# A list scheduler in the source that orders all engines between token tiles 2 and 95 of an attention and feed-forward kernel

## The chip, the cores and the metric

The kernel runs on one core of a Trainium2 chip. A core has a matrix engine (PE, with PEld for its weight loads), a vector engine (DVE), a scalar engine (ACT), GpSimd (POOL) and SyncE (SP), which issues nearly all DMA transfers here. Each engine works through its own list of instructions in the order of the program; an instruction whose inputs or buffers are not ready holds up everything behind it on its engine. The metric is the device time of one execution in microseconds (us). Before the change it is 1622.03 us, the median of three runs (1621.46 to 1624.27).

## What is computed

```python
# x: 4 x 12480 x 128, inducing: 32 x 128, w_in: 128 x 2048, w_out: 2048 x 128
def mab(q, kv):
    s = scale * (q @ kv.transpose(0, 2, 1))
    a = np.exp(s - s.max(-1, keepdims=True))
    a /= a.sum(-1, keepdims=True) + 1e-09
    return a @ kv
h = mab(I, x)          # 32 rows attend to all tokens of a batch
y = mab(x, h)          # each token attends to those 32 rows
z = y @ w_in
out = np.maximum(0.01 * z, z) @ w_out
```

## The kernel before, in words

**Tiles.** The 49920 tokens are cut into 98 tiles (`tiles`): 96 of 512 tokens and two of 384, which hold the ends of two batches each. A batch has six groups of 2048 tokens (four tiles each) and a rest of 192 (`GROUPS`).

**The main work.** A token's row of `y` is its 32 attention weights A times `h`, so z = A (h w_in), and the first product of the feed-forward part has a depth of 32 only. PE is therefore used as four independent row groups of 32 rows. One *slot* is one tile with one of the 16 column blocks f of z. It has three first products (`ffn_first`, weights `hwhi`, `hwlo`, data `A4`; high and low halves of fp32 numbers) on row group f % 4, into a PSUM bank `ph`; then ACT writes `ghi` = relu (L853) and DVE `glo`, the low half (L856), and after that the bank is free. For every fourth f (`FAR`) ACT writes `g` (L846), which frees the bank, and POOL makes `ghi` and `glo` from it (L848, L849). Then come twelve second products, three on each row group, each with its own accumulator bank. All of these go through `quarter` (L878). A tile is 16 slots and three linear products (the 0.01 z part): 243 products. At its end `gather` adds the four banks (ACT copy L1160, DVE sum L1163, POOL sum L1167) and `store` transposes (L924) and writes out.

**The side work** prepares the next batch and the next A: loads of x (`xc` L321, `xr` L311), DVE transposes into `xT` (L440), scores for `h` (L335, L347, L366), values (L486, L459), the weights' product (L655), and for each group `second` (L335, then DVE, POOL and ACT on `y`) and `stack`: ACT casts A to `both` (L736), POOL makes its low half (L741), and SP copies it to the four row groups of `A4` (L755). `both` has one buffer, so the next cast needs all four tiles' copies out of it done. The side products use all 128 rows of PE; such a stretch between two L878 products is called a *cluster* here.

**What sets the order.** Tiles 0, 1 and 97 run on the whole array (L904). For tiles 2 to 96 four generators (`row_group`) take turns, one product each. `row_group` sets a place for each slot's first products, `AHEAD` = 4 slots ahead of its second products (8 for `FAR`), row group r lags by r slots, and `glo` is issued `LATER` = 4 turns after `ghi`. Once per slot `next_slot` steps each lane of the side work by one piece (`others`), and `cluster` issues waiting side products when one has waited 10 slots. PSUM banks come from one list of eight, freed after a fixed number of turns. No durations are known to it.

## Time and profile before

| | |
|---|---|
| median of three runs | 1622.03 us |
| the profiled execution's own time | 1625.5 us |
| its span, first to last instruction | 1623.7 us |
| mean granted TensorE clock | 0.984 |
| DVE busy | 1157.0 us (71%) |
| ACT busy | 1068.4 us (66%) |
| POOL busy | 943.3 us (58%) |
| the chain that ended last | PE 82%, DVE 6%, POOL 4%, issue 3%, ACT 2% |

A row of a timeline has the start in us from the span's start, the duration in us, engine, line, operation, output<-inputs and shapes; in brackets stands how long the engine sat idle before it, and what ended that. A row of the waits names the waiting instruction, the one that released it, the sum in us, how often, and the longest. PE's matmuls are pipelined: one row group starts a product about every 0.23 us, while each row shows about 0.39 us. A few matmul records are missing from the trace.

### The profile page before, as it was taken

The page shows a single profiled execution, that of the slowest core. Times are in us where ns is not written, and L with a number is a line of the kernel's source. Part 1 is how long each engine was busy: PE and PEld are TensorE (multiplying, and loading weights), DVE is VectorE, ACT ScalarE, POOL GpSimd, SP SyncE. Part 2 cuts the span into 40 slices and gives each one's busy share as a digit, 9 for nine tenths or more (in the row PEclk, how much of TensorE's full clock was granted, in tenths as well). Part 3 has the DMA queues.
Part 4 walks back from the last instruction along what each step waited for, and adds up shares of the span by engine and source line. Part 5 has one row for each costly group of instructions (what it writes and reads, how often), then busy time and mean ns, then how long its engine had stood idle before and what let it go on. Part 6 is the DMA issues. An engine that isn't in the chain of part 4 may idle for free.

```text
span 1623.7 us, 59550 instructions
## 1 busy us (share of the span) xinstructions
PE 1571.7 (97%) x25047; PEld 1339.5 (82%) x25047; DVE 1157.0 (71%) x2046; ACT 1068.4 (66%) x1957; POOL 943.3 (58%) x963
## 2 busy tenths in 40 slices
PE   7999999999989999999998999999999999999997
PEld 5678777787877888888887878887888899999996
DVE  6677778767767777867675778776767676776764
ACT  6456656666756667766675567666666667777773
POOL 2046555556656655556665565655666666666663
PEclk9899999999999999999999999999999999999998
DMA  7154545522354446423225346542222232333321
GB/s 263 16 112 84 109 94 94 117 56 46 59 107 75 86 90 141 113 48 58 48 57 109 72 97 124 107 111 48 53 58 44 49 63 52 57 58 61 61 48 21
DMA packets 400700, 128.46 MB, mean 79 GB/s; under 512 B 373136, under 2 KB 375600, under 8 KB 400432
## 3 DMA queue, kind: packets, MB, share of 16 engines
q1 hardware_dynamic: 399328, 124.50, 38.0%
q8 instruction: 197, 3.23, 0.8%
q14 instruction: 71, 0.58, 0.1%
q10 hardware_dynamic: 1104, 0.15, 0.1%
HBM read 48.94 MB, written 25.56 MB: 46 GB/s over the span
## 4 chain that ended last, share of the span: by engine, by line
PE 82%; DVE 6%; POOL 4%; issue 3%; ACT 2%; SPq 1%; DMA 1%; ACTq 0%; DVEq 0%; POOLq 0%
PE bank L878 75%; PE bank L335 3%; DVE glo L856 2%; POOL glo L849 2%; PE bank L904 2%; PE bank L459 1%; POOL ghi L848 1%; DVE part L1163 1%; SPq L755 1%; ACT ghi L853 1%; DMA A<-both 1%; POOL y L710 1%; PE bank L366 0%; POOL y L696 0%; DVE e L347 0%
## 5 line engine op out<-in xcount | busy, mean ns | idle before, releaser
L878 PE MATMUL bank<-ghi,w_hi 32*128 32x512 f32 (+1 forms) x6080 | 1294.8, 393 | 2.2 <-DVE glo L856 1.7
L878 PE MATMUL bank<-glo,w_hi 32*128 32x512 f32 x6080 | 1293.9, 393 | 0.2 <-DVE glo L856 0.2
L878 PE MATMUL bank<-ghi,w_lo 32*128 32x512 f32 (+1 forms) x6080 | 1292.0, 393 | 0.0
L878 PE MATMUL bank<-A,hwhi 32*128 32x512 f32 (+1 forms) x3394 | 1140.0, 394 | 28.8 <-DVE glo L856 15.4
L856 DVE SCALAR_TENSOR_TENSOR glo<-bank,ghi 128x512 fp32r<-128x512 f32 x1184 | 792.4, 680 | 306.4 <-ACT ghi L853 301.0
L853 ACT ACTIVATE ghi<-bank 128x512 fp32r<-128x512 f32 x1184 | 703.1, 598 | 325.2 <-PE bank L878 306.6
L878 PEld LDWEIGHTS bank<-ghi,w_hi 32*128 32x128 f32 x6080 | 842.1, 184 | 51.1 <-issue 14.3
L878 PEld LDWEIGHTS bank<-ghi,w_lo 32*128 32x128 f32 x6080 | 847.4, 184 | 27.8
L878 PEld LDWEIGHTS bank<-glo,w_hi 32*128 32x128 f32 x6080 | 843.6, 184 | 28.6 <-DVE glo L856 0.6
L878 PEld LDWEIGHTS bank<-A,hwhi 32*128 32x128 f32 x3394 | 581.0, 185 | 90.1 <-DVE glo L856 42.4
L878 PE MATMUL bank<-A,hwlo 32*128 32x512 f32 (+1 forms) x1697 | 640.2, 390 | 0.0
L849 POOL TENSOR_TENSOR glo<-g,ghi 128x512 fp32r<-128x512 f32 (+1 forms) x384 | 495.9, 1291 | 30.7
L848 POOL CAST ghi<-g 128x512 fp32r<-128x512 f32 (+1 forms) x384 | 234.6, 611 | 417.2 <-ACT g L846 356.8
L878 PEld LDWEIGHTS bank<-A,hwlo 32*128 32x128 f32 x1697 | 305.8, 185 | 8.3
L846 ACT ACTIVATE g<-bank 128x512 f32<-128x512 f32 (+1 forms) x384 | 229.4, 597 | 124.8 <-PE bank L878 120.6
L1167 POOL TENSOR_TENSOR part<-part 128x512 f32<-128x512 f32 (+1 forms) x95 | 122.6, 1291 | 103.9 <-DVE part L1163 103.9
L1163 DVE TENSOR_TENSOR part<-bank,part 128x512 f32<-128x512 f32 (+1 forms) x190 | 129.2, 680 | 33.5 <-PE bank L878 21.0
L1160 ACT COPY part<-bank 128x512 f32<-128x512 f32 (+1 forms) x190 | 110.5, 581 | 26.1 <-PE bank L878 24.8
L924 DVE STREAM_TRANSPOSE osb<-part 128x512 f32<-128x512 f32 (+1 forms) x95 | 65.9, 694 | 0.0
L440 DVE STREAM_TRANSPOSE xT<-xc 128x512 f32<-128x512 f32 x72 | 50.2, 697 | 0.0
L741 POOL TENSOR_TENSOR both<-aT,both 128x512 fp32r<-128x512 f32 x24 | 31.1, 1295 | 29.2 <-ACT both L736 25.1
L690 DVE STREAM_TRANSPOSE y<-bank 128x512 f32<-128x512 f32 (+1 forms) x28 | 18.1, 647 | 21.3 <-PE bank L335 21.3
(120 smaller groups left out, 643.6 us busy)
## 6 DMA issues: line engine op xcount, KB each, us to landing
A<-both SPq DMA_DIRECT2D x376, 128.0 KB, 2.4
xr<-in_x_dram SPq DMA_DIRECT2D x96, 256.0 KB, 4.7
out_dram<-osb SPq DMA_DIRECT2D x382, 64.0 KB, 2.3
xc<-in_x_dram SPq DMA_DIRECT2D x288, 64.0 KB, 2.7
raw<-in_moe_w_in_dram SPq DMA_DIRECT2D x4, 512.0 KB, 6.6
raw<-in_moe_w_out_dram SPq DMA_DIRECT2D x4, 512.0 KB, 7.5
A<-both SPq DMA_DIRECT2D x48, 16.0 KB, 1.8
out_dram<-osb SPq DMA_DIRECT2D x48, 8.0 KB, 1.8
```

Source lines behind the costliest of these rows:

```text
L335: nc.tensor.matmul(dst, lhsT, rhs, start=True, stop=True)
L440: nc.vector.transpose(t[:, j, :], blk.rearrange("p n c -> p (n c)"))
L846: nc.scalar.activation(g[:, :n], ph[:, :n], AF.Relu)
L848: nc.gpsimd.tensor_copy(ghi[:, :n], g[:, :n])
L849: nc.gpsimd.tensor_tensor(out=glo[:, :n], in0=g[:, :n], in1=ghi[:, :n].bitcast(F32), op=ALU.subtract)
L853: nc.scalar.activation(ghi[:, :n], ph[:, :n], AF.Relu)
L856: nc.vector.scalar_tensor_tensor(out=glo[:, :n], in0=ph[:, :n], scalar=0.0, in1=ghi[:, :n].bitcast(F32), op0=ALU.max, op1=ALU.subtract,)
L878: nc.tensor.matmul(dst, w[32 * r : 32 * r + 32], x[32 * r : 32 * r + 32], start=start, stop=stop, tile_position=(32 * r, 0),)
L924: nc.vector.transpose(osb[:, :n], total[:, :n])
L1160: nc.scalar.copy(part[:, :n], po[:, :n])
L1163: nc.vector.tensor_tensor(out=part[:, :n], in0=po[:, :n], in1=part[:, :n], op=ALU.add)
L1167: nc.gpsimd.tensor_tensor(out=total[:, :n], in0=total[:, :n], in1=part[:, :n], op=ALU.add)
```

## The change

The kernel's arithmetic and its instructions' shapes stay. Between tiles 2 and 96 the fixed slots go, and a list scheduler that runs while the program is written takes their place. It keeps a clock for ACT, DVE, POOL and SP, the time at which each row group is free, the time at which each bank comes free, and the estimated end of each DMA, all in ns from constants in the source. At each step it takes what can start first: a product (`option`), a queued job of an engine (`best`), or a piece of a side lane, which gives way to queued jobs by `YIELDING`. First products may run up to ten slots ahead (`GB` = 10 buffers of `ghi` and of `glo`; before 7 and, for `FAR`, 3). Which slots go to POOL is no longer every fourth: `relu` sends a slot there when POOL would be done 1200 ns ahead of need. Side products are put in by `clustered`, by age or when PE would idle. `quarter` is L988 now, relu L975, `glo` on DVE L978 and on POOL L1216 and L1218, the cast to `both` L856.

```diff
-    FAR = 3
-    XB = 3
-    LATER = 4
-    FURTHER = 4
-    GB = 7
-    AHEAD = 4
-    LAG = 1
+    GB = 10
+    SLOT = 868.0
+    QUARTER = 231.6
+    SIGNAL = 35.0
+    DRAINED = 200.0
+    TURNED = 200.0
+    LANDED = 2300.0
+    RELU, LOW, COPIED, ADDED, BLOCKS = 599.0, 690.0, 585.0, 685.0, 700.0
+    FAR_HIGH, FAR_LOW, FAR_SUM = 611.0, 1291.0, 1291.0
+    EARLY, PREFER, YIELDING, PATIENCE = 1200.0, 0.0, 200.0, 15000.0
...
+    def spent(engine, ns, *after):
+        if not quads[0]:
+            return 0.0
+        clock[engine] = max([clock[engine], now[0], *(a + SIGNAL for a in after)]) + ns
+        return clock[engine]
...
     def stack(tiles_, eng=None):
...
+        when = max(landed.get("both", 0.0), *(landed.get((b, g, "aT"), 0.0) for b, g in at))
+        yield from new(ACT, when)
...
                     for r in range(4):
                         nc.sync.dma_start(
...
+                        landed["A", t] = landed["both"] = spent(SP, 640.0, when) + LANDED
...
-        if quads[0]:
-            events.append((turn[0] + LATER, rest))
...
+        def relu(i, ph, ready):
+            t, f = work[i]
+            _, n = spans(t)
+            ghi, glo = live[t, f]
+            start = max(clock[ACT], ready + SIGNAL)
+            far = max(clock[POOL], start + RELU) + backlog(POOL) + FAR_HIGH + FAR_LOW
+            left = far_ends[-2] if len(far_ends) > 1 else 0.0
+            wanted = now[0] + (i - turn_of[0]) * SLOT - EARLY
+            if far_open[0] < 2 and left <= start and far <= wanted:
+                g = sb.tile([P, TOK], F32, tag="g", name="g", bufs=2)
+                high(ph, g, n)
...
+                add(POOL, at, FAR_HIGH + FAR_LOW, on_pool)
                 return
...
+            high(ph, ghi, n)
+            high_at[i] = at = spent(ACT, RELU, ready)
...
+            add(DVE, at, LOW, rest)
...
+            i = firsts[0]
+            if i < len(work) and i % 4 == r and i - min(turn_of) < GB:
...
+                    at = max(rows[r], at + SIGNAL)
+                    if not found or at <= found[0][0] + PREFER:
+                        return at, "first"
...
+        def best(engine):
+            found = None
+            for j in jobs[engine]:
+                if j[3] is None or j[3]():
+                    start = max(clock[engine], j[0] + SIGNAL)
+                    if found is None or start < found[0]:
+                        found = start, j, None
+            for k, (e, at) in enumerate(asks):
+                if e == engine and lanes[k]:
+                    start = max(clock[engine], at + SIGNAL)
+                    if found is None or start + YIELDING < found[0] or (
+                        found[2] is not None and start < found[0]
+                    ) or start - at > PATIENCE and start <= found[0]:
+                        found = start, None, k
+            return found
...
+            if (
+                start == math.inf
+                or any(ages[k] > patience(k) for k in ready)
+                or len(ready) > 1 and max(ages.values()) > PAIRED
+                or start > min(rows) + IDLE
+            ):
...
-        streams = [row_group(r) for r in range(4)]
-        while streams:
-            streams = [m for m in streams if next(m, StopIteration) is not StopIteration]
-            turn[0] += 1
-            happen(turn[0])
-        happen(math.inf)
+        while min(turn_of) < len(work):
+            turn_over()
+        while any(jobs.values()) or NT - 1 not in A4:
+            turn_over(False)
```

The last tile's work is now written ahead of the store of tile 96, and not around it.

What that does to the order is shown at three places. The number in a name counts tiles in the order in which the program made them, over all engines.

The first place is the cast to `both` for one group of tiles in the third batch, on ACT. Before, with the copies that it has to wait for, on SP:

```order
L941 DMA out_0_dram<-osb_18184 512x1x32 x4
L321 DMA xc_18519<-in_x_dram 32x16x32 x8
L755 DMA A4_18699<-both_17315 32x1024 x4
L941 DMA out_0_dram<-osb_18575 512x1x32 x4
L755 DMA A4_19061<-both_18736 32x1024 x4
```

```order
L853 ACTIVATE ghi_18684<-bank1_65 128x512
L853 ACTIVATE ghi_18710<-bank2_66 128x512
L853 ACTIVATE ghi_18726<-bank3_67 128x512
L736 CAST both_18736<-aT_16629 128x512
L846 ACTIVATE g_18767<-bank1_65 128x512
L853 ACTIVATE ghi_18780<-bank2_66 128x512
```

After, the last copy out of the earlier `both`, on SP, and the cast, on ACT:

```order
L878 DMA A4_18807<-both_17544 32x1024 x4
L1054 DMA out_0_dram<-osb_18899 512x1x32 x4
```

```order
L975 ACTIVATE ghi_18809<-bank1_65 128x512
L975 ACTIVATE ghi_18822<-bank5_69 128x512
L975 ACTIVATE ghi_18843<-bank2_66 128x512
L975 ACTIVATE g_18893<-bank6_70 128x512
L975 ACTIVATE ghi_18884<-bank1_65 128x512
L975 ACTIVATE g_18934<-bank5_69 128x512
L975 ACTIVATE ghi_18927<-bank2_66 128x512
L975 ACTIVATE g_18985<-bank6_70 128x512
L975 ACTIVATE ghi_18976<-bank5_69 128x512
L975 ACTIVATE ghi_18993<-bank1_65 128x512
L975 ACTIVATE g_19033<-bank2_66 128x512
L856 CAST both_19051<-aT_15549 128x512
```

Before, two activations of relu (`ghi_18710`, `ghi_18726`) are made between the copy `A4_18699` and the cast `both_18736`; after, eleven (`ghi_18809` to `g_19033`) are made between `A4_18807` and `both_19051`. Over all groups of these tiles the count before is 2, but for three groups (15, 6 and 7); after, leaving out the first group, it is 4 to 24, with a median of 8.

The second place is DVE some eight tiles into this part, while the second batch's scores run (`e`, `rm`, `rd`, `least`, `nm`, `zs` and `ay` are steps of the next batch's `h`; `xT` its transposed tokens; `y`, `mx` steps of the next A). Before:

```order
L378 TENSOR_SCALAR least_3166,nm_3165<-bank2_66,nm_2153 128x4
L690 STREAM_TRANSPOSE y_3172<-bank0_64 128x512
L856 SCALAR_TENSOR_TENSOR glo_3145<-bank3_67,ghi_3144 128x512
L856 SCALAR_TENSOR_TENSOR glo_3181<-bank1_65,ghi_3180 128x512
L694 TENSOR_REDUCE mx_3206<-y_3172 128x16
L856 SCALAR_TENSOR_TENSOR glo_3197<-bank3_67,ghi_3196 128x512
L856 SCALAR_TENSOR_TENSOR glo_3240<-bank2_66,ghi_3239 128x512
L400 TENSOR_SCALAR zs_3275<-zs_2274,al_3255,zg_3257 128x1
L486 STREAM_TRANSPOSE ay_3277<-e_2866 128x512
```

After:

```order
L978 SCALAR_TENSOR_TENSOR glo_3049<-bank2_66,ghi_3048 128x512
L447 TENSOR_SCALAR zs_3099<-zs_1999,al_2698,zg_2700 128x1
L794 STREAM_TRANSPOSE y_3102<-bank5_69 128x512
L567 STREAM_TRANSPOSE ay_3114<-e_2303 128x512
L800 TENSOR_REDUCE mx_3130<-y_3102 128x16
L420 TENSOR_SCALAR least_3149,nm_3148<-bank6_70,nm_2569 128x4
L385 TENSOR_SCALAR e_3155,rm_3156<-bank0_64 128x512
L398 TENSOR_SCALAR rd_3158,any_3159<-own_75,rm_3156 128x4
L495 STREAM_TRANSPOSE xT_3161<-xc_2597 128x512 x2
L978 SCALAR_TENSOR_TENSOR glo_3137<-bank5_69,ghi_3136 128x512
```

Before, one or two pieces of side work stand between two `glo`; after, a run of nine instructions does. The change has four runs of side work on DVE longer than 3.0 us by the trace's durations, all in the stretches where a batch's scores and values are made; before has none.

The third place is POOL in the second half of the program, from a tile's sum (`part`) on. Before:

```order
L1167 TENSOR_TENSOR part_21889<-part_21889,part_21935 128x512
L848 CAST ghi_21977<-g_21979 128x512
L849 TENSOR_TENSOR glo_21978<-g_21979,ghi_21977 128x512
L848 CAST ghi_22060<-g_22062 128x512
L849 TENSOR_TENSOR glo_22061<-g_22062,ghi_22060 128x512
L848 CAST ghi_22150<-g_22152 128x512
L849 TENSOR_TENSOR glo_22151<-g_22152,ghi_22150 128x512
L848 CAST ghi_22234<-g_22236 128x512
L849 TENSOR_TENSOR glo_22235<-g_22236,ghi_22234 128x512
L1167 TENSOR_TENSOR part_22243<-part_22243,part_22283 128x512
```

After:

```order
L1261 TENSOR_TENSOR part_22612<-part_22612,part_22645 128x512
L1216 CAST ghi_22668<-g_22691 128x512
L1218 TENSOR_TENSOR glo_22669<-g_22691,ghi_22668 128x512
L1216 CAST ghi_22712<-g_22740 128x512
L1218 TENSOR_TENSOR glo_22713<-g_22740,ghi_22712 128x512
L1216 CAST ghi_22768<-g_22792 128x512
L1218 TENSOR_TENSOR glo_22769<-g_22792,ghi_22768 128x512
L1216 CAST ghi_22814<-g_22840 128x512
L1218 TENSOR_TENSOR glo_22815<-g_22840,ghi_22814 128x512
L1216 CAST ghi_22878<-g_22902 128x512
L1218 TENSOR_TENSOR glo_22879<-g_22902,ghi_22878 128x512
L826 TENSOR_TENSOR y_22354<-y_22354,sm_22561 128x512
```

Before, four slots of a tile (a CAST and a TENSOR_TENSOR each) stand between two sums; after, five to seven. Over the program, POOL takes 516 slots and not 384, and DVE 1052 and not 1184. The clusters on PE between tiles 2 and 96 are 78 and not 68, with nearly the same side products in them.

More of the change, by code (lines that the diff above doesn't have):

```diff
@@ L67, in induced_attention_then_leaky_ffn @@
     HEAVY = 2
-    FAR = 3
-    XB = 3
-    QUIET = range(4)
-    LATER = 4
-    FURTHER = 4
-    ON_PE = "pe"
+    PE, ACT, DVE, POOL, SP = "PE", "ACT", "DVE", "POOL", "SP"
     LOADS = [2, 6, 10, 14, 18]
@@ L124, in done, with on_array, old, new @@
         if quads[0]:
-            free.append((turn[0] + later, i))
-            free.sort()
+            free.append((at, i))
+    clock = {ACT: 0.0, DVE: 0.0, POOL: 0.0, SP: 0.0}
+    rows = [0.0] * 4
+    tiling = ["f"]
+    now = [0.0]
+    def spent(engine, ns, *after):
[3 more added lines that the diff above has]
+        return clock[engine]
+    def on_array(kind, ns, *after):
+        if not quads[0]:
+            return 0.0
+        start = max(*rows, now[0], *(a + SIGNAL for a in after)) + (tiling[0] != kind) * TURNED / (
+            1 if "r" in (kind, tiling[0]) else 2
+        )
+        tiling[0] = kind
+        rows[:] = [start + ns] * 4
+        return start + ns + DRAINED
+    def old(debt_=0):
+        if not quads[0]:
+            yield debt_
+    def new(engine, at=0.0):
+        if quads[0]:
+            yield engine, at
+    def until(test, engine=None):
+        while not test():
+            yield (engine, now[0] + 300.0) if quads[0] else None
     def aux_ps(name):
@@ L361, in running @@
         )
-        yield HEAVY
+        at = spent(DVE, 305.0)
+        yield from old(HEAVY)
         if b:
-            yield ON_PE
+            yield from new(PE, at)
         pm = aux_ps("mx_ps")
@@ L368, in running @@
         )
+        at = on_array("f", 64.0, at, taken[0])
         if not b:
             yield
+        yield from new(DVE, at)
         nm_old = maxima.get(b)
@@ L381, in running @@
             )
-        done(pm)
+        at = spent(DVE, 305.0, at)
+        done(pm, at)
         maxima[b] = nm
-        yield
+        yield from old()
+        yield from new(ACT, at)
         if nm_old is not None:
@@ L417, in first_scores @@
         for _ in range(3):
+            yield from new(SP)
             more()
-        yield from idle(4)
+        if not quads[0]:
+            yield from idle(4)
         for g in [RG, *range(RG)]:
             _, J, K = GROUPS[g]
-            w, rows = 32 * K, 32 * J
+            w = 32 * K
             if g == RG:
@@ L715, in second @@
+        yield from old()
+        yield from old()
+        yield from new(DVE, at)
         if g == RG:
@@ L736, in stack @@
             nc.scalar.copy(ahi[: 32 * J, o : o + 32 * K], aT[b, g][: 32 * J, :])
-        yield
+        when = spent(ACT, 620.0, when)
+        yield from old()
+        yield from new(POOL, when)
         for (b, g), o in at.items():
@@ L753, in stack @@
                 for j in js:
+                    yield from new(SP, when)
                     for r in range(4):
@@ L1153, in gather, with add @@
-        def gather(t, r):
+        free.extend((0.0, i) for i in range(8) if i not in held)
+        lanes = [stacking, stores, seconds, values, middles, scores]
+        asks = [(None, 0.0)] * len(lanes)
+        jobs = {ACT: [], DVE: [], POOL: []}
+        work = [(t, f) for t in range(QUICK, NT - 1) for f in range(NF)]
+        turn_of, product_of = [0] * 4, [0] * 4
+        firsts, running_first = [0], [None] * 4
+        high_at, low_at = {}, {}
+        far_ends, far_open = [], [0]
+        def add(engine, ready, ns, emit, allowed=None):
+            jobs[engine].append((ready, ns, emit, allowed))
@@ L1164, in gather, with summed @@
-            done(po)
+                parts_of[t, r] = part, spent(ACT, COPIED, ready)
+                done(po, clock[ACT])
+            def summed():
+                part, at = parts_of[t, r - 1]
+                nc.vector.tensor_tensor(out=part[:, :n], in0=po[:, :n], in1=part[:, :n], op=ALU.add)
+                at = spent(DVE, ADDED, ready, at)
+                parts_of[t, r] = part, at
+                done(po, at)
+                if r == 3:
+                    add(POOL, at, FAR_SUM, joined, lambda: (t, 1) in parts_of)
@@ new lines, in joined @@
+            def joined():
+                (total, first_at), (part, at) = parts_of[t, 1], parts_of[t, 3]
+                for q in range(4):
+                    del parts_of[t, q]
+                nc.gpsimd.tensor_tensor(out=total[:, :n], in0=total[:, :n], in1=part[:, :n], op=ALU.add)
+                at = spent(POOL, FAR_SUM, at, first_at)
+                stores.append(store(t, total, True, at))
+            if r % 2:
+                add(DVE, ready, ADDED, summed, lambda: (t, r - 1) in parts_of)
+            elif r:
+                add(ACT, ready, COPIED, copied, lambda: (t, 0) in parts_of)
+            else:
+                add(ACT, ready, COPIED, copied, lambda: not parts_used[0])
@@ L1177, in induced_attention_then_leaky_ffn, with products @@
-        happen(math.inf)
+        def products(t, f, r):
+            parts, n = spans(t)
+            ghi, glo = live[t, f]
+            made = [
+                (w[:, f, :], x[:, :n], 0, n, k) for k, (w, x) in enumerate(((w_hi, ghi), (w_lo, ghi), (w_hi, glo)))
+            ]
+            if f == LINEAR and r != t % 4:
+                k = (r - t) % 4 - 1
+                made = [
+                    (hw[b][1 + k % 2][:, TOK:], A4[t][:, k // 2, o : o + w], o, w, b) for b, o, w in parts
+                ] + made
+            return made
```

592 lines of the change are left out of this document (365 added, 227 removed).

## The prediction, made before the changed kernel ran

> **What bounds the kernel now.** The groups of the page come first.
>
> ```profile
> PE 1571.7 (97%) x25047; PEld 1339.5 (82%) x25047; DVE 1157.0 (71%) x2046; ACT 1068.4 (66%) x1957; POOL 943.3 (58%) x963
> L878 PE MATMUL bank<-A,hwhi 32*128 32x512 f32 (+1 forms) x3394 | 1140.0, 394 | 28.8 <-DVE glo L856 15.4
> L856 DVE SCALAR_TENSOR_TENSOR glo<-bank,ghi 128x512 fp32r<-128x512 f32 x1184 | 792.4, 680 | 306.4 <-ACT ghi L853 301.0
> L853 ACT ACTIVATE ghi<-bank 128x512 fp32r<-128x512 f32 x1184 | 703.1, 598 | 325.2 <-PE bank L878 306.6
> ```
>
> PE is the bound, and its idle time stands almost wholly ahead of first products, which need a free bank. How much is lost is read from the windows: first all of the part between tiles 2 and 96, then ten undisturbed tiles, then four places to which I come (columns: us, busy of PE, PEld, DVE, ACT, POOL, granted clock, DMA share, GB/s).
>
> ```profile
> 103.30:1596.60 1493.30, 1463.31 (x24206) 1264.69 (x24206) 1080.83 (x1851) 1006.72 (x1830) 914.80 (x934) 0.99 0.39 76
> 1427.00:1568.00 141.00, 141.00 (x2423) 133.52 (x2420) 98.85 (x151) 102.16 (x181) 90.59 (x92) 1.00 0.30 58
> 229.50:235.00 5.50, 4.56 (x52) 3.71 (x56) 4.07 (x9) 1.71 (x4) 2.91 (x4) 0.69 0.33 72
> 486.00:494.00 8.00, 5.66 (x39) 2.99 (x43) 2.67 (x5) 3.10 (x8) 4.37 (x6) 0.57 0.38 64
> 889.00:900.00 11.00, 8.31 (x63) 5.04 (x67) 4.22 (x8) 4.37 (x8) 5.59 (x6) 0.53 0.46 91
> 1295.00:1300.00 5.00, 4.84 (x52) 4.05 (x56) 4.42 (x9) 3.29 (x7) 2.13 (x3) 0.66 0.57 121
> ```
>
> The rate comes from one copy and the same copy ten tiles on, in the ACT timeline:
>
> ```profile
> 1426.87 0.58 ACT L1160 COPY part<-bank 128x512 f32<-128x512 f32 x1
> 1568.50 0.58 ACT L1160 COPY part<-bank 128x512 f32<-128x512 f32 x1
> ```
>
> That is 14.16 us a tile, 0.0583 for each of its 243 products, 0.233 for a row group's next one. The 93 full tiles and two of 384 tokens (10.6 each) need 1338.1 us. The 68 clusters add the time between the L878 products around each. The first and the last are
>
> ```profile
> 124.07 0.40 PE L878 MATMUL bank<-ghi,w_lo 32*128 32x512 f32 x1
> 126.46 0.49 PE L878 MATMUL bank<-ghi,w_hi 32*128 32x512 f32 x1
> ...
> 1311.10 0.27 PE L878 MATMUL bank<-A,hwhi 32*128 32x192 f32 x1
> 1312.29 0.35 PE L878 MATMUL bank<-A,hwhi 32*128 32x192 f32 x1
> ```
>
> (2.39 and 1.19 us), and all 68 sum to 97.6. So 1493.3 − 1338.1 − 97.6 = 57.6 us are lost: PE idle is 1493.30 − 1463.31 = 30.0 of it, the half clock about 12 (5.5 × 0.31 + 8 × 0.43 + 11 × 0.47 + 5 × 0.34), the rest short unevenness. An order cannot win much more than these 57.6 us.
>
> The largest loss is a chain on SP and ACT. One of its four places, in the timelines of SP, ACT and PE:
>
> ```profile
> 879.95 6.16 SPq L321 DMA_DIRECT2D xc<-in_x_dram  x8
> 886.21 2.48 SPq L755 DMA_DIRECT2D A<-both  x4
> 890.53 0.62 ACT L736 CAST both<-aT 128x512 fp32r<-128x512 f32 x1 [8.18 <-DMA A<-both]
> 885.91 0.39 PE L878 MATMUL bank<-glo,w_hi 32*128 32x512 f32 x2
> 891.69 0.79 PE L878 MATMUL bank<-A,hwhi 32*128 32x512 f32 x1 [5.39 <-ACT g L846]
> ```
>
> The copies into A4 stand on SP behind eight loads of xc; the cast needs the one buffer `both`, which these copies still read; ACT, in order, idles 8.18 us ahead of the cast with relus queued behind it, no bank comes free, and PE goes from 885.91 to 891.69 without a product. The same happens here:
>
> ```profile
> 482.68 0.38 PE L878 MATMUL bank<-ghi,w_hi 32*128 32x512 f32 x1
> 488.34 0.79 PE L878 MATMUL bank<-A,hwhi 32*128 32x512 f32 x1 [5.25 <-ACT g L846]
> ...
> 1291.35 0.39 PE L878 MATMUL bank<-ghi,w_lo 32*128 32x512 f32 x1
> 1295.16 0.49 PE L878 MATMUL bank<-A,hwhi 32*128 32x512 f32 x1 [3.42 <-DVE glo L856]
> ...
> 229.03 0.39 PE L878 MATMUL bank<-ghi,w_lo 32*128 32x512 f32 x1
> 230.44 0.61 PE L878 MATMUL bank<-A,hwhi 32*128 32x512 f32 x1 [1.02 <-DVE glo L856]
> ```
>
> **The change, part by part.** *Cast.* The new order puts a median of 8 relus (4 to 24) after the last A4 copy ahead of the cast, where mostly 2 stood. Eight relus are about half a tile, 7 us, as the kernel makes 16 in 14.16; SP's 8.6 us of issues in the rows above then lie beside relus already written. I take the four stalls (5.6 + 5.7 + 3.7 + 1.4 = 16.4) and the half clock behind them (12) as gone: **−29 us**, with 0.6 lost just ahead of the 229.03 one. At the places with only 4 relus, half might come back: −15 to −29.
>
> *Other bank and `glo` waits.* 25 more gaps of over 0.35 us between L878 products are released by `glo` on DVE; the first and the last are
>
> ```profile
> 187.32 0.39 PE L878 MATMUL bank<-ghi,w_hi 32*128 32x512 f32 x1
> 188.53 0.49 PE L878 MATMUL bank<-A,hwhi 32*128 32x512 f32 x1 [0.82 <-DVE glo L856]
> ...
> 1231.52 0.39 PE L878 MATMUL bank<-ghi,w_lo 32*128 32x512 f32 x1
> 1232.64 0.49 PE L878 MATMUL bank<-ghi,w_hi 32*128 32x512 f32 x1 [0.72 <-DVE glo L856]
> ```
>
> Above the usual 0.06 between starts they sum to **−20 us**. They come from a fixed lead of some 54 to 68 products between the last first product of a slot and the first use of its `ghi`, by the order, into which side work falls at any time; the new lead is 66 to 98 outside the crowded stretches. I count all of them as gone, and those that take their place in the next step.
>
> *Crowded stretches.* While a batch's scores and values run, the new order writes DVE's side work in longer runs (four over 3.0 us, eleven over 2.5; before none and two), and 53 slots have leads of 40 products or less (38 of 35 or less). A slot needs a relu (0.598) and a `glo` (0.680) and hand-overs, some 1.8 us or 31 products. DVE catches up slowly once late:
>
> ```profile
> 892.16 1.88 DVE L856 SCALAR_TENSOR_TENSOR glo<-bank,ghi 128x512 fp32r<-128x512 f32 x3 [8.54 <-ACT ghi L853]
> ```
>
> three `glo` in 1.88 us, 0.63 each. Moreover the new order itself leaves row groups out: walking through PE's list with 0.0583 between starts and 0.233 before a row group's next product loses 8.6 us in these stretches (before 0), and in the two narrow tiles and at the end 12 against 11. A product that stands fewer than four places behind the last one of its row group waits for it, and 228 do here. To the 8.6 I add 6 for late `glo`, 0.16 for each of the 38 slots, a quarter of a `glo`, since most are short by a few products only: **+15 us and +1**. Bounds of the late part: 0 (the lead suffices) and 53 × 0.68 = 36 (each waits a whole `glo` more).
>
> *POOL.* It takes 516 slots, not 384; nearly all the extra ones stand in the three quiet stretches, 270 pairs of CAST and TENSOR_TENSOR there. Their pace, in POOL's timeline:
>
> ```profile
> 1401.40 0.61 POOL L848 CAST ghi<-g 128x512 fp32r<-128x512 f32 x1
> 1402.10 1.30 POOL L849 TENSOR_TENSOR glo<-g,ghi 128x512 fp32r<-128x512 f32 x1
> ...
> 1404.95 1.29 POOL L849 TENSOR_TENSOR glo<-g,ghi 128x512 fp32r<-128x512 f32 x1
> 1406.20 1.30 POOL L741 TENSOR_TENSOR both<-aT,both 128x512 fp32r<-128x512 f32 x1
> ```
>
> 0.70 + 1.25 = 1.95 a pair from start to start. With the sums and y, POOL's work there is 627 us, PE's own 627 with its clusters. POOL is no longer spare in these stretches; what it runs late waits for PE's ten buffers. I take **+5 us**, near the lower end, as a slot goes to POOL only where ten buffers leave it time; 0 if the lead absorbs all of it, +32 if each of the 270 pairs costs 0.12 more than in these rows. DVE's relief (132 × 0.68 = 90 us) wins nothing: in the calm window DVE is busy 98.85 of 141.
>
> *Clusters.* 78 and not 68, with almost the same products; priced piece by piece from the gaps of before, **+2.5 us** (0 if those put in where PE idles cost nothing, +12 if the extra ten cost 1.2 each, as the last one above).
>
> *DMA.* The source counts 2.3 us from issue to landing:
>
> ```profile
> A<-both SPq DMA_DIRECT2D x376, 128.0 KB, 2.4
> ```
>
> The median is 2.4, and eight loads of xc are still one piece on SP, so that copies moved behind them leave up to 6.16 us late. A cast whose `both` or a first product whose A4 comes late holds ACT or PE with all that is queued behind it. Three A4 buffers cover most of that: **+2 us** (0 to 8, half of the 16.4 from before).
>
> *Tail.* The stores of tile 96 now stand behind tile 97's work:
>
> ```profile
> 1618.55 0.72 DVE L924 STREAM_TRANSPOSE osb<-bank 128x512 f32<-128x512 f32 x1 [4.16 <-PE bank L913]
> ```
>
> DVE had idled 4.16 us there, which hides the transpose; 0, at worst SP's 2.5 us for four issues.
>
> *Sum* against the profiled run's own 1625.5: − 29 − 20 + 15 + 1 + 5 + 2.5 + 2 = 1602.0. That run stands 3.5 above the median of 1622.03, so **1598.5, say 1599 us**.
>
> *A rule weighed.* Half clock follows 5.6 us of standstill (0.57, 0.53), and also the 1.4 us at 229.03 (0.69). The Trainium skill, "TensorE: Matmul & The Clock Gate", section "Part 1: The HAM clock gate (the "warmup" mystery)", says that the clock halves after an idle window of about 3.4 us; the 229.03 case disagrees, as it is shorter. By that rule alone no new half clock would come here; by the rows it can, which is a rival below.
>
> **Rivals.** (1) *No new stalls*: only −29 − 20 + 2.5: 1579 against the profile, **1575.5**. For it: longer leads on most slots; against: the row groups that the order itself leaves out. (2) *POOL paces PE* in the quiet stretches: +32 in place of +5, **1626**. For it: 627 against 627; against: the source sends a slot to POOL only if it will be done 1.2 us early. (3) *Slower: late `glo` in the crowded stretches.* DVE's runs of side work hold `glo`, the list is in order on PE, and all four row groups stop. Without the late part the sum is 1593; at a whole `glo` for each of the 53 slots it is 1593 + 36 = **1629**; it decides from 32/53 = 0.6 us a slot. For it: leads down at 31 products; against: 38 of the 53 are short by a few products only. (4) *Half clock.* If each of the eleven DVE runs over 2.5 us makes a pause that halves the clock as at 229.03 (1.7 us there), +19, less the 6 already counted: **1612**. The Trainium skill, same page, section "A second HAM failure mode: psum-queue depth-cycling", tells of a clock that swings when PE pauses often between bursts of bank use; the trace shows it once, at 229.50. (5) *The order moves, the time doesn't*: the waits go to other instructions, **1622 to 1625**. Against it: the cast's wait has no second cause in the rows.
>
> **How the numbers follow.** Forecast with its neighbourhood, 1586 to 1608: 0.58. (1) 0.19, (2) 0.05, (3) 0.08, (4) 0.07, (5) 0.03. The range from 1573 to 1617 takes in the forecast, (1) and (4) and leaves (2), (3) and (5) out. A bound of 0.2% (3.2 us) is about what a measurement of this kernel can tell from no change. Faster: 0.58 + 0.19 + 0.07 = 0.84; within: (5) and part of (2), 0.05; slower: (3) and the rest of (2), 0.11.
>
> **What would show it.** Right: the wait of ACT's cast for DMA A<-both shrinks from 8.18 to under 2 us, PE has no gap over 2 us, the granted clock is over 0.95 in all windows, calm tiles stay at 14.16 us, and the gaps that remain ahead of L988 products lie where scores and values run, near 180 to 270, 490 to 680 and 880 to 1040 us. POOL is busy over 95% in the quiet stretches without PE waiting for its `glo`. Wrong: calm tiles over 14.3 us (POOL), PE gaps over 1 us by the dozen in the crowded stretches (rival 3), a clock under 0.8 anywhere (rival 4), or casts that still hold ACT.

## The result, and the profile after

| | before | after |
|---|---|---|
| median | 1621.74 us (4 runs, 1620.03 to 1624.27) | 1604.57 us (4 runs, 1600.74 to 1607.09) |
| ratio | | 0.9891 (95% interval 0.9864 to 0.9917) |
| the profiled execution's own time, and its span | 1625.5, 1623.7 us | 1606.44, 1604.7 us |
| mean granted clock | 0.984 | 0.986 |

The change makes the kernel 1.1% faster. The page of the changed kernel, the lines that answer to those of before:

```profile
PE 1565.6 (98%) x25047; PEld 1360.7 (85%) x25047; DVE 1084.6 (68%) x1914; ACT 1080.4 (67%) x1957; POOL 1179.3 (73%) x1227
L988 PE MATMUL bank<-A,hwhi 32*128 32x512 f32 (+1 forms) x3394 | 1051.6, 392 | 9.1 <-ACT g L975 3.6
L978 DVE SCALAR_TENSOR_TENSOR glo<-bank,ghi 128x512 fp32r<-128x512 f32 (+1 forms) x1052 | 697.3, 682 | 362.9 <-ACT ghi L975 345.3
```

The idle time ahead of first products fell from 28.8 to 9.1 us, and yet the clock hardly moved. The windows tell why (columns as before): three quiet stretches (the third takes in the last cast place, tiles 74 to 76), and two short ones where new stalls stand.

```profile
300.00:450.00 150.00, 150.00 (x2525) 139.52 (x2521) 97.54 (x155) 109.13 (x191) 143.12 (x151) 1.00 0.29 55
700.00:850.00 150.00, 150.00 (x2534) 138.40 (x2530) 100.06 (x157) 109.43 (x194) 142.51 (x150) 1.00 0.30 58
1180.00:1480.00 300.00, 300.00 (x5204) 280.10 (x5200) 201.47 (x315) 220.85 (x390) 243.88 (x255) 1.00 0.30 57
567.60:574.40 6.80, 5.44 (x52) 4.33 (x56) 2.54 (x4) 3.94 (x9) 3.79 (x4) 0.50 0.10 15
635.80:642.60 6.80, 5.95 (x60) 4.19 (x64) 2.16 (x5) 1.79 (x3) 0.00 (x0) 0.50 0.94 209
```

In these stretches PE has no idle time at all, with POOL busy for 143 of 150 us in the first two and for 244 of 300 in the third. New half clock has come elsewhere.

**Where the time went, stretch by stretch.** The first ACT copy of a tile (L1160 before, L1244 after) marks the same point of the work in both traces. Tile 25 and tile 34, before and after:

```profile
497.50 0.56 ACT L1160 COPY part<-bank 128x512 f32<-128x512 f32 x1
641.07 0.59 ACT L1160 COPY part<-bank 128x512 f32<-128x512 f32 x1 [0.48 <-PE bank L878]
```

```profile
488.78 0.59 ACT L1244 COPY part<-bank 128x512 f32<-128x512 f32 x1 [0.39 <-PE bank L988]
651.09 0.58 ACT L1244 COPY part<-bank 128x512 f32<-128x512 f32 x1
```

So these nine tiles took 143.6 us and take 162.3. The same for all stretches; clusters are the time between the products around them, half clock is half the time at granted clock 0.5, gaps are PE pauses over 0.47 us outside clusters, without what the half clock adds to them (all in us):

| copy of tile to copy of tile | before | after | difference | clusters | half clock | gaps |
|---|---|---|---|---|---|---|
| 99.7 us to 2 (handover) | 18.9 | 26.6 | +7.7 | −0.4 | +1.7 | +4.3 |
| 2 to 10 (scores, values) | 132.2 | 139.1 | +6.9 | +8.9 | −1.7 | −3.1 |
| 10 to 24 (quiet) | 220.7 | 206.1 | −14.6 | −10.0 | 0 | −3.2 |
| 24 to 25 (cast) | 26.0 | 17.3 | −8.7 | −1.6 | −3.4 | −5.1 |
| 25 to 34 (scores, values) | 143.6 | 162.3 | +18.7 | +9.7 | +6.8 | +3.9 |
| 34 to 49 (quiet) | 233.5 | 223.8 | −9.7 | −3.9 | 0 | −3.8 |
| 49 to 50 (cast) | 27.3 | 15.4 | −12.0 | −2.9 | −5.1 | −6.9 |
| 50 to 59 (scores, values) | 140.9 | 162.6 | +21.7 | +17.6 | +1.7 | +0.7 |
| 59 to 74 (quiet) | 233.5 | 217.9 | −15.6 | −10.5 | 0 | −5.2 |
| 74 to 76 (cast) | 35.0 | 28.1 | −6.9 | −1.1 | −1.7 | −4.0 |
| 76 to 96 | 282.5 | 281.2 | −1.3 | +1.2 | 0 | 0 |
| 96 to the end | 29.8 | 24.7 | −5.1 | | | |

The cast places win 27.6 us, the quiet stretches 39.9 and the tail 5.1; the crowded stretches give back 47.3 and the handover 7.7. Much of the middle is only moved: 24.4 us of clusters left the quiet stretches and 36.2 came into the crowded ones, 9 of these being waits (below).

**The handover.** The last copies out of the earlier `both` on SP, the cast on ACT, then PE:

```profile
99.86 2.42 SPq L878 DMA_DIRECT2D A<-both  x4
107.13 0.62 ACT L856 CAST both<-aT 128x512 fp32r<-128x512 f32 x1 [9.55 <-DMA out_dram<-osb]
108.29 0.79 PE L988 MATMUL bank<-ghi,w_hi 32*128 32x512 f32 x1 [4.80 <-ACT ghi L975]
```

The first cast of the new order stands ahead of every relu of tile 2 (0 relus between the last A4 copy and it, before 15). The last of the four copies landed at 106.87 us, which fits the cast's start; the profile names one of the stores behind them. PE waits from 103.10 to 108.29, and the granted clock is 0.5 for 6.8 us from 106.8 on.

**A cast that is late again**, on ACT and SP:

```profile
567.79 0.62 ACT L856 CAST both<-aT 128x512 fp32r<-128x512 f32 x1 [4.42 <-DMA out_dram<-osb]
554.55 8.50 SPq L1054 DMA_DIRECT2D out_dram<-osb  x12
563.15 2.46 SPq L878 DMA_DIRECT2D A<-both  x4
```

SP issued the copies out of `both` only from 563.15 to 565.6 us, behind twelve stores; the last of them landed at 567.5, which fits the cast's start, though the profile names a store. PE stood for 3.7 us.

**A value product whose xr is late**, on PE and on SP:

```profile
632.15 0.38 PE L406 MATMUL bank<-rd,e 128*128 128x4 f32 x2
632.47 0.42 PE L535 MATMUL bank<-xr,ay 128*32 128x128 f32 x8
635.29 0.43 PE L535 MATMUL bank<-xr,ay 128*32 128x128 f32 x8 [2.40 <-DMA xr<-in_x_dram]
635.92 0.66 PE L535 MATMUL bank<-xr,ay 128*32 128x128 f32 x8 [0.20 <-DMA xr<-in_x_dram]
637.30 0.66 PE L535 MATMUL bank<-xr,ay 128*32 128x128 f32 x8 [0.73 <-DMA xr<-in_x_dram]
637.89 0.79 PE L988 MATMUL bank<-A,hwlo 32*128 32x512 f32 x1
...
617.89 7.40 SPq L357 DMA_DIRECT2D xc<-in_x_dram  x8
625.39 3.40 SPq L878 DMA_DIRECT2D A<-both  x4
631.58 2.05 SPq L346 DMA_DIRECT2D xr<-in_x_dram  x4
```

PE began the cluster at 632 us with data whose load SP had issued only at 631.58. A cluster holds up all four row groups; this one took 6.06 us, the one at 955 us 5.90 and the one at 994 us 2.92, where 1.9 would be usual for these products (0.64 for the two on L406, 1.33 for the 32 on L535, as other clusters show): 9.2 us too much, of it 1.5 by half clock inside the clusters, and more half clock behind two of them.

**The scheduler's own clock.** The source keeps a time for each instruction that it writes; printed and put beside the trace, it shows where the chip leaves the plan. At the copy of tile 2 the chip is 6.0 us behind, at tile 24 6.7, at tile 34 25.2, at tile 49 26.7, at tile 59 35.5, at tile 95 40.1. So the quiet parts are planned right to about 1 us in ten tiles, and the rest is lost at the handover, where the clocks start at zero while the engines still have work, and in the crowded stretches. There SP is planned without a pause. Between 450 and 600 us it makes 205 issues, 0.73 us each; the source counts 0.64 to 0.675 (xr 0.49). SP's own lag grows from 7 us at 457 to 27 us at 627, and what needs its data waits.

### The profile page after: what moved, and what is told of

It is laid out like the page before. It is cut to its first block, busy times and chain, and to the rows that moved or that the text cites. A ratio compares the mean times of both kernels' runs of the same rounds, so it can differ in the third digit from the quotient of the medians.

```text
span 1604.7 us, 60005 instructions
## 1 busy us (share of the span) xinstructions
PE 1565.6 (98%) x25047; PEld 1360.7 (85%) x25047; DVE 1084.6 (68%) x1914; ACT 1080.4 (67%) x1957; POOL 1179.3 (73%) x1227
## 4 chain that ended last, share of the span: by engine, by line
PE 89%; SPq 4%; DMA 4%; DVE 2%; issue 1%; ACT 1%; POOL 0%; ACTq 0%; DVEq 0%; POOLq 0%
PE bank L988 83%; PE bank L372 2%; DMA xr<-in_x_dram 2%; SPq L878 2%; SPq L357 1%; PE bank L1018 1%; PE bank L535 1%; DVE glo L978 1%; DMA raw<-in_moe_w_in_dram 1%; SPq L346 0%; DMA A<-both 0%; POOL glo L1218 0%; ACT ghi L975 0%; PE bank L406 0%; DMA out_dram<-osb 0%
## 5 line engine op out<-in xcount | busy, mean ns | idle before, releaser
L988 PE MATMUL bank<-ghi,w_hi 32*128 32x512 f32 (+1 forms) x6080 | 1221.3, 393 | 4.8 <-ACT ghi L975 4.8
L988 PE MATMUL bank<-ghi,w_lo 32*128 32x512 f32 (+1 forms) x6080 | 1214.6, 392 | 0.0
L988 PE MATMUL bank<-glo,w_hi 32*128 32x512 f32 (+1 forms) x6080 | 1213.7, 392 | 0.0
L988 PE MATMUL bank<-A,hwhi 32*128 32x512 f32 (+1 forms) x3394 | 1051.6, 392 | 9.1 <-ACT g L975 3.6
L978 DVE SCALAR_TENSOR_TENSOR glo<-bank,ghi 128x512 fp32r<-128x512 f32 (+1 forms) x1052 | 697.3, 682 | 362.9 <-ACT ghi L975 345.3
L988 PEld LDWEIGHTS bank<-ghi,w_hi 32*128 32x128 f32 x6080 | 775.4, 184 | 42.9 <-ACT ghi L975 6.0
L988 PEld LDWEIGHTS bank<-glo,w_hi 32*128 32x128 f32 x6080 | 770.0, 184 | 35.2 <-issue 9.8
L988 PEld LDWEIGHTS bank<-ghi,w_lo 32*128 32x128 f32 x6080 | 773.4, 184 | 31.0 <-issue 5.8
L975 ACT ACTIVATE ghi<-bank 128x512 fp32r<-128x512 f32 (+1 forms) x1052 | 611.5, 598 | 217.4 <-PE bank L988 187.6
L1218 POOL TENSOR_TENSOR glo<-g,ghi 128x512 fp32r<-128x512 f32 (+1 forms) x516 | 668.1, 1295 | 41.3
L988 PE MATMUL bank<-A,hwlo 32*128 32x512 f32 (+1 forms) x1697 | 621.6, 390 | 0.0
L988 PEld LDWEIGHTS bank<-A,hwhi 32*128 32x128 f32 x3394 | 569.1, 184 | 38.1 <-DVE glo L978 7.3
L975 ACT ACTIVATE g<-bank 128x512 f32<-128x512 f32 (+1 forms) x516 | 308.6, 598 | 210.2 <-PE bank L988 174.3
L1216 POOL CAST ghi<-g 128x512 fp32r<-128x512 f32 (+1 forms) x516 | 316.4, 613 | 135.6 <-ACT g L975 96.0
L988 PEld LDWEIGHTS bank<-A,hwlo 32*128 32x128 f32 x1697 | 302.5, 184 | 6.2 <-issue 1.4
L1244 ACT COPY part<-bank 128x512 f32<-128x512 f32 (+1 forms) x190 | 110.4, 583 | 18.1 <-PE bank L988 14.9
L1037 DVE STREAM_TRANSPOSE osb<-part 128x512 f32<-128x512 f32 (+1 forms) x95 | 66.6, 701 | 11.2 <-POOL part L1261 10.5
```

The lines of the kernel that those rows point to most:

```text
L975: nc.scalar.activation(ghi[:, :n], ph[:, :n], AF.Relu)
L978: nc.vector.scalar_tensor_tensor(out=glo[:, :n], in0=ph[:, :n], scalar=0.0, in1=ghi[:, :n].bitcast(F32), op0=ALU.max, op1=ALU.subtract,)
L988: nc.tensor.matmul(dst, w[32 * r : 32 * r + 32], x[32 * r : 32 * r + 32], start=start, stop=stop, tile_position=(32 * r, 0),)
L1037: nc.vector.transpose(osb[:, :n], total[:, :n])
L1216: nc.gpsimd.tensor_copy(ghi[:, :n], g[:, :n])
L1218: nc.gpsimd.tensor_tensor(out=glo[:, :n], in0=g[:, :n], in1=ghi[:, :n].bitcast(F32), op=ALU.subtract)
```

## The experiments

All ratios are to the kernel before, run on the same chip.

### The cast alone: b_cast

```diff
 # before.py, stack()
+        if quads[0]:
+            yield from idle(6)
         both = sb.tile([P, 2, TOK], F32R, tag="both", name="both", bufs=1)
```

> The kernel before, with the cast to both held back by six more slots (8 relus after the last A4 copy instead of 2), nothing else. If the stalls of 3.7 to 5.7 us and the half clock behind them come from the cast standing too early on ACT, the time falls by 20 to 29 us (to 1593 to 1602) and ACT's waits of 8 us for DMA A<-both go. Rival: the stall only moves, because the A4 copies themselves come late on SP; then the first products wait for A<-both instead and the time falls by less than 8 us.

Measured: 1599.97 us, ratio 0.9866 (0.9848 to 0.9885). ACT's wait in the waits of before, then, of b_cast, one of the cast places, the same wait and a window:

```profile
ACT both L736 <- DMA A<-both: 23.7, 5, 8.2
```

```profile
879.31 0.62 ACT L738 CAST both<-aT 128x512 fp32r<-128x512 f32 x1 [1.54 <-DMA A<-both]
...
ACT both L738 <- DMA A<-both: 2.7, 2, 1.5
...
885.00:896.00 11.00, 11.00 (x189) 10.29 (x185) 10.02 (x18) 7.73 (x14) 8.28 (x9) 1.00 0.22 34
```

ACT's wait for the copies went from 23.7 to 2.7 us in all, the clock of that place from 0.53 to 1.00. In the stretch table b_cast wins 7.4, 7.9 and 4.0 us at the three cast places and 1.6 and 1.5 us in tiles 2 to 10 and 10 to 24; every other stretch stays within 0.8 us. The cast's place alone wins 21 us, at least as much as the whole change (17 us; the two intervals of the ratios overlap).

### How late may it stand: b_cast10

As b_best below, with `idle(10)`: sixteen relus after the last copy.

> The kernel before with the two edits of b_best, the cast ten slots later and not six. If PE's remaining gaps at the three cast places (1.5, 2.7 and 1.1 us) are still the cast waiting for A4's copies, 2 to 4 us more are won: 1592 to 1595. Rival: six slots already cover the copies and the gaps are DVE's glo behind side work; then the time stays at 1596 to 1597, or A4 comes late and it rises.

Measured: 1615.57 us, ratio 0.9965 (0.9950 to 0.9980): the rival's last clause. The waits, ACT and SP rows of its trace:

```profile
PE bank L880 <- DMA A<-both: 13.5, 3, 5.7
...
124.05 0.61 ACT L738 CAST both<-aT 128x512 fp32r<-128x512 f32 x1
...
117.47 8.30 SPq L321 DMA_DIRECT2D xc<-in_x_dram  x11
125.81 0.62 SPq L311 DMA_DIRECT2D xr<-in_x_dram  x1
131.01 4.98 SPq L757 DMA_DIRECT2D A<-both  x8
```

Now PE waits three times for A4 itself. Of the three places tried, two relus are too few, eight serve and sixteen are too many; the first costs 21 us and the last 19.

### The handover: a_entry and a_start

```diff
 # after.py; a_entry has the first line, a_start both
+        landed["both"] = 9000.0
+        clock.update({ACT: 2000.0, DVE: 6000.0, SP: 9000.0})
         free.extend((0.0, i) for i in range(8) if i not in held)
```

> The changed kernel, with the scheduler told at its start that both is still being read for 9 us; the first cast then stands behind 16 relus, not ahead of all of them. If the empty clocks at the handover cause PE's first stall (5.1 us at 103 us) and the half clock behind it, 6 to 8 us go (to 1597 to 1599). Rival: PE waits there for something else (DVE's side work, the copies of A4); then the stall stays and the time stays within 2 us.

Measured: 1607.97 us, 0.9913 (0.9888 to 0.9938); the handover took 24.0 us, not 26.6. The cast's stall went and PE then stood for another reason, DVE and PE rows:

```profile
100.75 0.65 DVE L818 TENSOR_REDUCE sm<-y 128x16 f32<-128x512 f32 x1
...
105.47 0.67 DVE L800 TENSOR_REDUCE mx<-y 128x16 f32<-128x512 f32 x1
...
106.79 0.79 PE L988 MATMUL bank<-glo,w_hi 32*128 32x512 f32 x1 [1.23 <-DVE glo L978]
```

Side work from 100.75 to 106.1 us stands ahead of DVE's first `glo`. So the handover got 2.6 us shorter, and what is left is the rival's. The whole did not fall as expected: it is no faster than the change, as tiles 25 to 34 take 171.0 us in this order (162.3 in the change).

> The changed kernel, with the scheduler's clocks at the handover not at zero but at ACT 2, DVE 6 and SP 9 us, and both in use until 9 us. With the cast alone moved (a_entry) PE still stood because nine pieces of DVE's side work came ahead of its first glo. If the empty clocks are the cause, the first copy of tile 2 starts at 118 to 121 us, as in the kernel before (118.6), not at 126, and 5 to 8 us are won up to there; the later stretches change by up to 10 us either way, as with every edit so far. Rival: DVE's side work at this place was already written before the scheduler starts; then 124 to 126 stays.

Measured: tile 2's copy comes at 120.5 us and not 126.3, as expected; the whole takes 1616.21 us (0.9977, 0.9963 to 0.9992) and is slower than the change. The stretch from 50 to 59 now takes 166.2 us (162.6 in the change), and one new stall behind tile 76 with its half clock makes 293.1 of 281.2 us. A scheduler that starts from other times deals out another order everywhere.

### SP's data: a_xr, a_sp, a_pace

```diff
 # a_xr
-        landed[b, g, q] = spent(SP, 490.0) + LANDED
+        landed[b, g, q] = spent(SP, 490.0) + 7000.0
 # a_sp
-        landed[b, g, q] = spent(SP, 490.0) + LANDED
+        landed[b, g, q] = spent(SP, 540.0) + 4600.0
-                at = spent(SP, 670.0)
+                at = spent(SP, 750.0)
-                        landed["A", t] = landed["both"] = spent(SP, 640.0, when) + LANDED
+                        landed["A", t] = landed["both"] = spent(SP, 750.0, when) + LANDED
-                    spent(SP, 675.0, at)
+                    spent(SP, 750.0, at)
 # a_pace
-                    yield from new(SP, at)
+                    yield from new(SP, max(at, paced[0]))
+                    paced[0] = now[0] + 14000.0
                     more()
```

> The changed kernel, with the estimate from issue to landing of xr raised from 2.3 to 7.0 us. If clusters at 632, 955 and 994 us are long (6.1, 5.9, 2.9 us) because a value product is put in before its xr has landed, these waits (9 us) and the half clock behind two of them (5 us) go: 1590 to 1596. Rival: xr is late because SP's list is, whatever landing is assumed; then the waits shift to other value products and less than 4 us is won.

Measured: 1619.09 us, 0.9991 (0.9973 to 1.0008). Clusters of 7.2, 3.4 and 4.3 us still wait for xr: a later landing alone does not help when the issue itself comes late. The rival held, and the new order is slower than the change's by 14 us, 12 of them in tiles 2 to 10 (151.0 us).

> The changed kernel, with the scheduler's prices for SP set to what SP's own rows show while it is full (0.75 us for an issue of xc, out and A4 instead of 0.64 to 0.675, xr 0.54) and 4.6 us from issue to landing of xr. If SP falls behind the scheduler's clock (by some 14 us between 440 and 600 us) and this is what makes the casts and value products of the crowded stretches late, the waits of PE for xr (16 us), the stall at 565 us and their half clock go: 1586 to 1596. Rival: any new constant only deals the same losses out anew; then the time stays between 1600 and 1615.

Measured: 1603.51 us, 0.9894 (0.9870 to 0.9918). PE's wait for xr, in the change and in a_sp, and a window of a_sp:

```profile
PE bank L535 <- DMA xr<-in_x_dram: 7.0, 7, 2.4
```

```profile
PE bank L535 <- DMA xr<-in_x_dram: 1.3, 1, 1.3
...
500.00:640.00 140.00, 139.04 (x2314) 121.44 (x2311) 113.79 (x208) 92.74 (x175) 50.21 (x51) 1.00 0.50 91
```

Stalls and half clock of the crowded stretches are gone, as the theory has it: tiles 25 to 34 take 145.7 us (162.3 in the change, 143.6 before), 50 to 59 153.3 (162.6, 140.9 before). But the time is the same, since tiles 2 to 10 take 146.0 and not 139.1 and the three quiet stretches 662.5 and not 647.7. The plan says why: honest prices make it longer by 25 us (1453 against 1428 to tile 95), and the chip keeps to it (11 us behind at tile 95, not 40). The change's plan was short because it was wrong.

> The changed kernel, with at least 14 us between two pieces of eight loads of xc, so that SP is no longer full while a batch's scores run; no price is touched. If the full SP queue is the cause, the crowded stretches (tiles 24 to 34 and 50 to 59) lose their surplus over the kernel before, some 19 and 22 us, and the quiet ones get a part of the clusters back (about 12 us): 1580 to 1594. Rival: what costs there is DVE's runs of side work or the clusters as such, not SP; then the losses follow the side work and the time stays over 1600.

Measured: 1605.89 us, 0.9905 (0.9878 to 0.9933). Tiles 2 to 10 and 50 to 59 come to 127.7 and 144.7 us, below or near the kernel before; tiles 25 to 34 only to 155.1, with short waits for A4 near 519 us and 10.2 us of half clock behind them. The quiet stretches take most of it back, 23.2 us (17.3 of it clusters that stand there again, where 12 were expected), and the tiles behind 76 another 9.8 (291.0 us).

### POOL's share and the lead: a_pool, a_gb7

```diff
 # a_pool
-            if far_open[0] < 2 and left <= start and far <= wanted:
+            if f % 4 == 3 and far_open[0] < 2 and left <= start and far <= wanted:
 # a_gb7
-            if i < len(work) and i % 4 == r and i - min(turn_of) < GB:
+            if i < len(work) and i % 4 == r and i - min(turn_of) < 7:
```

> The changed kernel, with POOL limited to every fourth slot, as before (384 at most and not 516). If POOL's larger share costs 5 us in the quiet stretches, as the prediction had it, 3 to 5 us are won there (tiles 10 to 24, 36 to 49, 60 to 74); if it costs nothing, the quiet tiles stay at 14.2 us and only the crowded stretches change, in either direction by up to 10 us. Rival: POOL's share is what relieves DVE, and taking it away brings bank waits back: quiet tiles get slower by 0.3 us or more, 12 us in all.

Measured: 1620.19 us, 1.0001 (0.9990 to 1.0012), with 233 slots on POOL. A quiet window of it:

```profile
1100.00:1250.00 150.00, 150.00 (x2530) 137.22 (x2526) 114.04 (x181) 109.09 (x192) 92.33 (x94) 1.00 0.30 56
```

PE is as full as with POOL at 143 of 150 us. The three quiet stretches are 10.3 us longer than in the change, but 9.0 of it is clusters that stand elsewhere in this order; POOL's share as such is worth about 1 us there. Of the crowded ones, tiles 2 to 10 and 25 to 34 are together 10 us longer and 50 to 59 8.4 us shorter.

> The changed kernel, with first products at most seven slots ahead, not ten. If the longer lead is what removed the bank and glo waits of the quiet stretches, PE's gaps over 0.4 us come back there (12 us before the change, 0 after) and the quiet stretches get slower by 5 to 12 us. Rival: the order by time does it, not the lead; then no such gaps come back and quiet tiles stay at 14.2 us.

Measured: 1652.93 us, 1.0201 (1.0182 to 1.0220). PE's last calm stretch in it:

```profile
1340.00:1620.00 280.00, 280.00 (x4703) 262.55 (x4701) 238.47 (x365) 201.37 (x351) 35.66 (x30) 1.00 0.29 55
```

Neither side held whole. Hardly any gaps come back in the quiet stretches (0.4 us in all), though the lead by the order is now 41 products in the median (63 before, 79 in the change). But a tile takes 14.5 us (290.3 for 20, 281.2 in the change), and PE shows no idle time: single row groups must run with pauses that the busy time does not show. With seven slots of lead hardly any slot passes the test for POOL (10 are left), so DVE takes all, and the run alone does not tell which of the two costs the 0.3 us a tile. A stretch of a_sp does, tiles 10 to 24, which have a median lead of 58 products and one slot on POOL:

```profile
290.00:440.00 150.00, 150.00 (x2496) 136.18 (x2493) 135.35 (x219) 109.48 (x192) 26.28 (x24) 1.00 0.29 55
```

These tiles have no gaps either and take 14.1 us each without the clusters, with DVE at 135 of 150 us. So DVE can take nearly all. A lead of 41 is too short for the full pace, 58 is enough, and the kernel before had gaps with its 63: it was not a longer lead that removed them, and the order by time is what is left to have done it.

### The tail: b_tail and b_best

```diff
 # b_tail, split_first() of before.py
-        if quads[0] and f % 4 == FAR:
+        if quads[0] and f % 4 == FAR and t < NT - 1:
 # b_best: b_cast, and in first_round()
             happen(math.inf)
+            turn[0] += 8 * quads[0]
```

> The kernel before, with the last tile (97) splitting all its slots on ACT and DVE, none on POOL, as the change does. If the tail's gain of 5 us in the changed kernel comes from POOL's slower slots at the start of tile 97 and the half clock after them, the time falls by 3 to 5 us (0.2 to 0.3%). Rival: the gain comes from the store of tile 96 standing behind tile 97; then nothing changes here (within 1 us).

Measured: 1622.99 us, 1.0010 (0.9995 to 1.0024): no gain, POOL's slots in tile 97 were not it.

> The kernel before with two edits: the cast six slots later (1600.0 us alone) and, in tile 97, banks taken in the order in which they came free, where the lowest number of the last four freed was taken until now. If the changed kernel's gain of 5 us in the tail comes from that, PE's waits of 2 to 3 us for glo in tile 97 and the half clock there go, and the time is 1594 to 1597, under both kernels. Rival: the tail's gain comes from the order of the last row groups' products; then it stays at 1600.

Measured: 1596.60 us, 0.9860 (0.9835 to 0.9885). PE's waits at the end, in b_tail, b_cast and b_best:

```profile
1594.76 0.79 PE L878 MATMUL bank<-A,hwhi 32*128 32x512 f32 x2 [3.04 <-DVE glo L856]
```

```profile
1575.12 0.89 PE L880 MATMUL bank<-A,hwhi 32*128 32x512 f32 x2 [1.84 <-DVE glo L858]
1579.06 0.79 PE L906 MATMUL bank<-ghi,w_hi 128*128 128x512 f32 x1 [2.19 <-DVE glo L858]
```

```profile
1573.99 0.64 PE L880 MATMUL bank<-A,hwhi 32*128 32x512 f32 x2 [1.84 <-DVE glo L858]
```

Before, the four banks freed last are taken again in each round of tile 97, since equal turns are sorted by the bank's number; with the oldest first, as the change does, the second wait goes and the stretch from tile 96 to the end falls from 29.8 to 25.6 us (24.7 in the change). The medians of b_cast and b_best alone would not tell them apart; the trace does.

### All three on the changed kernel: a_all

Edits of a_sp, a_pace and a_start together.

> The changed kernel with three edits together: SP's prices as in a_sp, 14 us between pieces of xc loads as in a_pace, and the clocks at the handover as in a_start. If the losses of the list scheduler are these three (entry 6, late SP data about 20, side work crowded together), they add up: 1582 to 1592, under the kernel before with its two edits (1596.6). Rival: the scheduler deals out new losses with every order, so that no sum holds; then 1596 to 1612.

Measured: 1595.13 us (1594.46 to 1597.57), 0.9842 (0.9826 to 0.9859). It beats the change by 9 us in the medians and by 0.5% in the ratios. The plan says 1444 us to tile 95 and the chip is 15.5 behind. It stops short of the expected sum: the crowded stretches win 37 us over the change and the handover 5.5, but the quiet stretches lose 25.7, and tiles 76 to 96 take 293.6 us (281.2 in the change), of it 3.4 half clock, 2.5 clusters and a stall. It cannot be told apart from b_best, two small edits to the kernel before.

## Why the prediction was right, and where it was not

1599 us was forecast, 1604.57 came, inside 1573 to 1617; the sum against the profile was −23.5 and −19.1 came. The number is better than the reasons. Two of the prediction's own signs of being wrong came true: the clock is 0.5 in four places between tiles 2 and 96, and casts still hold ACT (9.55, 5.00 and 4.42 us). PE has gaps of 4.8 and 3.4 us, where none over 2 was expected. Another sign held, that of calm tiles: they stay at 14.16 us, as the three quiet stretches without their clusters take 14.16, 14.15 and 14.15 a tile.

- **The cast (−29).** Right in mechanism: b_cast shows it alone at 21 us by the medians, 23.6 by the profiled executions. It was oversized by some 5 us, since smaller waits take the place (a wait of 1.6 us for A4 at 130 us, 1.5 us left at the cast). In the order in which the instructions are written, the relus ahead of a cast are 4 to 11, the first group left out, and not 4 to 24: a relu's buffer gets its number when its first products are written, before the relu itself. At the first place shown under "The change" they are seven and not eleven. The median is 8 either way.
- **Other bank and `glo` waits (−20).** The size was about right: 12.2 us of gaps went in the quiet stretches, and no such wait is left there; the gaps of before in tiles 2 to 10 and 25 to 34, another 7.0 us, went too, and others came. The reason given, the longer lead, failed: the gaps stay away with a lead of 41 products (a_gb7) and of 58 (a_sp), both shorter than before.
- **Crowded stretches (+15).** The sign was right and the cause wrong. DVE's late `glo` shows up as a single stall of over 0.5 us (0.79 at 519 us), and clusters, half clock and gaps explain all but 3 us of the 47, which leaves little for row groups left out and for shorter waits. Rival 3 had next to no part in it.
- **DMA (+2, at most 8).** This is the term that was mis-sized. Late SP data cost 9.2 us in clusters, 3.7 us at 565, 2.2 us in waits for A4 (514 to 517 us), and half clock of 3.4, 3.4 and 1.7, of which 2.2 fall into the clusters and the stall themselves: some 21 us. The working took the median landing of 2.4 us and did not ask how full SP's queue would be once the loads were written as early as possible.
- **The handover (not in the sum).** Measured +7.7, of it 1.7 half clock. The count of relus ahead of each cast was told "leaving out the first group"; that one group was where the cast stood too early.
- **POOL (+5).** 0, by a_pool, by tiles 10 to 24 of a_sp and by the calm tiles' 14.16 us. Rival 2 is out: POOL is busy for 95% of the first two windows, and PE is full.
- **Clusters (+2.5).** +7.0 in all, of it 9.2 of xr waits; without these −2.2. That they move into the crowded stretches was not foreseen.
- **Tail (0).** −5.1, of it 4.2 from the choice of banks (b_best); the rest stays open.
- **Half clock (rival 4).** It returned for 23.8 us, yet behind the stalls above and not behind DVE's runs. The Trainium skill's rule ("TensorE: Matmul & The Clock Gate", section "Part 1: The HAM clock gate (the "warmup" mystery)") of an idle window of about 3.4 us agrees with the handover, where half clock begins at 106.8 us after 3.3 us without a product. It is too strict for the others: at 567.6 us half clock begins after 2.0 us without one, and at 635.8 us pauses of 2.40 and 0.13 us inside one cluster had been enough.

So the sum came out near by luck: an overestimate on DVE and POOL stood in for the handover and SP. What stays open: how much of the new losses in tiles 2 to 10 is the moved clusters and how much PE's unevenness; and single edits to the scheduler's constants change every later decision, so that differences of about 10 us between a_entry, a_xr, a_start and a_pool belong to the whole new order and not to the edit alone. Only the stretches that an edit aims at were read as its effect.

## What to carry to other kernels

Count, for every instruction that waits for a transfer, how much of its engine's work is written between the end of that transfer's issue and the instruction; both sides have an edge, and one such place can be worth as much as a new order of everything. A scheduler that prices an issuing queue by the typical issue and starts with empty clocks plans work that the chip cannot keep: print its clock beside the trace, and the lag shows in minutes which price is wrong. When an order is made new, look at its first and its exceptional groups first.

## What the runs showed of the hardware

- From one issue on SP to the next it takes 0.63 to 0.67 us in the median (A4, xc, out), but 0.73 in the mean while SP is full (450 to 600 us of the changed kernel; xc and A4 0.75, out 0.71), as one xc issue in ten takes 1.1 us or more. It is the mean that counts for a queue without pauses.
- PE's busy time can be 100% and a tile still take 14.5 us in place of 14.2 (a_gb7): with four row groups a pause of one is not seen as idle time. Time per tile from marks in the trace is the sounder measure.
- Half clock begins only at points of a fixed grid: in the changed kernel between tiles 2 and 96 at 106.8, 567.6, 635.8 and 960.1 us, which lie 135, 20 and 95 steps of 3.413 us apart. Of the step just before each, PE had been without a product for 3.29, 2.01, 2.53 and 2.35 us; steps with up to 1.31 us left the clock at full in this run, while 1.27 us was enough at 230.7 us of the kernel before. So a pause's cost depends on where it falls, and no threshold follows from these runs.
